# The second block of 256 rows of an attention output stage: the plain form replaced by seven products

## The chip, the cores and the metric

The kernel runs on one core of a Trainium2 chip. The metric is the device time of the program in microseconds (us); three runs of the kernel before gave 1825.37, 1825.43 and 1826.04 us, with a median of 1825.43 us. A profile is one more execution, recorded by the hardware. Its engines are PE (TensorE, matmuls), PEld (its weight loads), DVE (VectorE), ACT (ScalarE), POOL (GpSimd) and SP (SyncE, which here only issues DMAs). L1521 means line 1521 of the kernel file.

## The reference, cut to what matters

The computation is a gated sum of an attention block and a mixture of small experts over 2048 tokens of width 1024:

```
qkv = x @ wqkv                       # 32 heads of 32
p   = softmax(q k^T / sqrt(32));  o = p v
a   = o.reshape(2048, 1024) @ wo     # the output projection
b   = sum over heads of gelu(x . u[e]) * v[e]   # e: one expert per head, by arg max
out = g * a + (1 - g) * b            # g = sigmoid(x . gate_w), one number per token
```

What the change touches is only the last step: `out`, rows by rows, from the unnormalised attention result `o`, a reciprocal per head and token (which has the gate in it), the weight `wo`, and a small second term (`at` times `vhl`) that carries `b`.

## The kernel before, in words

All large matmuls are made exact enough by splitting each float32 operand into a rounded high part and a low remainder; a product is then three matmuls, high with high, high with low and low with high. ACT makes the high part (a copy with rounding, L95) and DVE subtracts it from the operand to get the low part (L96). This pair is the function `split`.

The output stage works on eight blocks of 256 rows (`W = 256`), n = 0 to 7. For a block, `load_o` brings the attention result in as the tile `OC[n]` (128 partitions by 8 slices `kc` by 256 rows, in the pool `vpool`, name `V`, two buffers), and `load_rb` the reciprocals as `RB[n]` (name `accd`, two buffers; for block 0 the tile `rb0`). DVE multiplies the two (`scale_o`, L1575, or `split_o`, L1590).

There are two forms of the product of a block with `wo`:

- The plain form, `wo_mm`: for each of the 8 slices `kc`, three operand pairs by two row halves by two column halves, 12 matmuls (L1521), so 96 for a block, and 8 more matmuls (`av_mm`, L1528) for the second term. Blocks 0 and 1 use it. Its operands are `OH[n]` and `OL[n]` (tiles `z` and `acc`) and `woh[kc]`, `wol[kc]`.
- The form by seven products (Strassen-Winograd), `unit(n)`, for blocks 2 to 7. The block is cut into A11, A12, A21, A22 and the weight into B11 to B22. Seven products of 12 matmuls (`ht.product`, L964) and the same 8 matmuls of the second term, 92 in all. The operands are A11, A12, A22 and the sums S1 to S4 of rows, each 128 by 512, each made by `ht.operand`: for S1 to S4 a DVE sum (L946), then ACT high (L95) and DVE low (L96). On the weight's side they are B11, B21, B22, which lie in `woh` and `wol`, and T1 to T4, high and low parts of 1 MiB each, which were computed earlier, stored in device memory (`TD`) and loaded by `load_t`. P1 to P7 use the pairs (A11,B11), (A12,B21), (S4,B22), (A22,T4), (S1,T1), (S2,T2), (S3,T3). The results are added by DVE (`tt`, L970) in `post` (four slots of 512 columns; `post` is the tile `rb0` again) and in `c1`, and stored.

`unit(n)` also prepares the operands of block n + 1 (`ahead`) while PE works on block n, and loads block n + 2. P1 of the next block is the first to need them. PSUM has eight banks, taken in turn.

The order is written out by hand: every engine runs its instructions in the order of the program text, and no scheduler moves them. SP issues all loads and stores of this stage in that order too, so a DMA that has to wait for a buffer or for data holds back every DMA behind it. For the last attention head the row sums go to device memory and come back as reciprocals: `load_r` (rr from smd), `norm_r` (a reciprocal, then a store rd from rr), and then `load_chunk(n, KC - 1, KC)` loads the last slice (kc = 7) of o and of the reciprocals for blocks 0 and 1. PE does the slices 0 to 6 of block 0 in the meantime.

`plain_out(n, pa)` empties the four banks of a plain block into the four slots of `post`, DVE and ACT in turn, and issues one store of 256 KB from each slot.

Of the kernel before, what the change touches and what calls it, by code (L numbers as in the profile page):

```python
# [10 lines left out]
F32R = mybir.dt.float32r  # L11
# [5 lines left out]
S = 2048  # L17
D = 1024
H = 32
KC = D // 128  # L20
HC = KC // 2
# [3 lines left out]
W = 256  # L25
# [6 lines left out]
def gated_mha_peer_kernel(ctx, tc, xT, wqkv, wv, wo, wq, k12, ug, v, out):  # L32
# [869 lines left out]
    zp = Pool("zp", side="right")  # L902
# [66 lines left out]
    def tt(out, a, b, op=OP.add):  # L969
        nc.vector.tensor_tensor(out=out, in0=a, in1=b, op=op)  # L970
# [279 lines left out]
    keep = Pool("keep")  # L1250
# [157 lines left out]
    def load_o(n, k0, k1, queue=nc.sync):  # L1408
        if k0 == 0:
            OC[n] = vpool.tile([128, KC, W], F32, name="V")  # L1410
        dma(OC[n][:, k0:k1, :], OD[n // 2, :, :, n % 2, k0:k1, :].rearrange("d j g s -> (d j) g s"), queue)

    def load_rb(n, k0, k1, queue=nc.sync):
        if k0 == 0:
            RB[n] = rb0 if n == 0 else wk.tile([128, KC, W], F32, name="accd")
        src = RD[:, n, k0:k1, :].rearrange("j g s -> j (g s)")[None]
        dma(RB[n][:, k0:k1, :].rearrange("p g s -> p (g s)"),
            src.to_broadcast([32, 4, (k1 - k0) * W]), queue)
# [83 lines left out]
    fin = Pool("fin")  # L1502
# [9 lines left out]
    def load_at(n):  # L1512
        AT[n] = fin.tile([128, W], F32R, name="at", bufs=3)
        dma(AT[n], ATD[:, n * W:(n + 1) * W])

    def wo_mm(pa, n, kcs, first, last):
        for kc in kcs:
            wh, wl = (W0[0][:, 0], W0[0][:, 1]) if n == kc == 0 else (woh[kc], wol[kc])
            for a, b, i in ((OH[n], wh, 0), (OH[n], wl, 1), (OL[n], wh, 2)):
                for tt, half in pa:  # L1520
                    nc.tensor.matmul(pa[tt, half], a[:, kc, tt * 128:(tt + 1) * 128],  # L1521
                                     b[:, half * 512:(half + 1) * 512],
                                     start=(first and kc == kcs[0] and i == 0),
                                     stop=(last and kc == kcs[-1] and i == 2))

    def av_mm(n, tt, half, ps, first=False, last=False):
        for i in range(2):
            nc.tensor.matmul(ps, AT[n][:, tt * 128:(tt + 1) * 128],  # L1528
                             vhl[:, i, half * 512:(half + 1) * 512],
                             start=(first and i == 0), stop=(last and i == 1))  # L1530
# [8 lines left out]
    def store(n, tt, half, r, c=slice(0, 512)):  # L1539
        dma(out[n * W + tt * 128:n * W + (tt + 1) * 128, half * 512 + c.start:half * 512 + c.stop],  # L1540
            r[:, c])
# [18 lines left out]
    def load_t(i, *parts):  # L1560

        ops = ht.b.setdefault(f"T{i + 1}", [None, None])
        for n, (part, src) in enumerate(zip(parts, TD[i])):
            if part is None:
                continue
            m = HC // len(part)
            for j, place in enumerate(part):
                dma(place, src[:, m * j:m * j + m, :].rearrange("p k m -> p (k m)"))
            ops[n] = [place[:, k * 512:(k + 1) * 512] for place in part for k in range(m)]

    def scale_o(n):

        for k in range(2):
            o = OC[n][:, k * HC:(k + 1) * HC]
            nc.vector.tensor_mul(o, o, RB[n][:, k * HC:(k + 1) * HC])  # L1575
        ht.rows(OC[n])
# [3 lines left out]
    def plain_out(n, pa):  # L1580
        for i, ((j, half), ps) in enumerate(pa.items()):
            if i % 2:
                nc.scalar.activation(post[:, i], ps, AF.Copy)
            else:
                nc.vector.tensor_copy(post[:, i], ps)
            store(n, j, half, post[:, i])

    def split_o(n, k0, k1):
        o = OC[n][:, k0:k1, :]
        nc.vector.tensor_mul(o, o, RB[n][:, k0:k1, :])  # L1590
        split(OH[n][:, k0:k1, :], OL[n][:, k0:k1, :], o)

    def banks4():
        return {(i, half): bank() for i in range(W // 128) for half in range(2)}
# [8 lines left out]
    for kc in range(1, KC - 1):  # L1603
        split_hi(kc + 1)
        if kc == 1:
            norm_sums(H - 1, sm, nc.scalar)
            load_r(G - 1)
            for n in range(2):
                load_at(n)
            load_o(1, 0, KC - 1)  # L1610
            pso.close()
        split_lo(kc)
        wo_mm(pa, 0, [kc], False, False)
        if kc == HC:
            norm_r(G - 1)
    for n in range(2):
        load_chunk(n, KC - 1, KC)
    load_rb(2, 0, KC)
    split_lo(KC - 1)
    split(woh[0], wol[0], raw_wo(0))  # L1620

    load_t(2, None, [fin.tile([128, S], F32R, name="t3l")])
    OH[1] = zp.tile([128, KC, W], F32R, name="z1")
    OL[1] = wk.tile([128, KC, W], F32R, name="acc")
    split_o(1, 0, HC)
    split_o(0, KC - 1, KC)
    load_o(2, 0, KC)
    load_t(0, *([keep.tile([128, S], F32R, name=f"wo_raw{j}")] for j in range(2)))  # L1630
    ps_odd = Pool("ps_odd", space=PSUM)
    for (i, half), ps in pa.items():
        av_mm(0, i, half, ps)
    wo_mm(pa, 0, [KC - 1], False, True)
    split_o(1, HC, KC)
    load_at(2)
    load_t(2, [zp.tile([128, S], F32R, name="z0")], None)
    load_t(1, *([keep.tile([128, S], F32R, name=f"wo_raw{2 + j}")] for j in range(2)))
    load_rb(3, 0, KC)
    load_o(3, 0, KC)  # L1640
    pa1 = banks4()
    wo_mm(pa1, 1, list(range(KC - 1)), True, False)
    for (i, half), ps in pa1.items():
        av_mm(1, i, half, ps)
    plain_out(0, pa)
    load_t(3, *([part[k][:, 512:] for k in range(HC)] for part in (woh, wol)))
    ht.places(wk.tile([128, S], F32R, name="acc"), "A11", "A12")
    ht.places(fin.tile([128, S], F32R, name="s31"), "S3", "S1")
    scale_o(2)
    for name in ("A11", "S3", "S1", "A12"):  # L1650
        ht.operand(name)
    wo_mm(pa1, 1, [KC - 1], False, True)
    ht.places(zp.tile([128, S], F32R, name="z1"), "S2")
    ht.places(wk.tile([128, S], F32R, name="acc"), "S4", "A22")
    load_at(3)
    ht.b.update({f"B{i + 1}{j + 1}": [[part[i * HC + k][:, j * 512:(j + 1) * 512] for k in range(HC)]
                                    for part in (woh, wol)] for i in range(2) for j in range(2)})

    def osb():
        return wk.tile([128, 512], F32, name="osb")  # L1660
# [1 line left out]
    def unit(n):  # L1662


        u2, u3, u5 = (post[:, i] for i in range(3))
        last = n == S // W - 1

        def ahead(*names):
            if last:
                return  # L1670
            for name in names:
                if name == "A11":
                    scale_o(n + 1)
                ht.operand(name)

        p1 = ht.product("P1")
        c1 = osb()
        nc.scalar.activation(c1, p1, AF.Copy)
        if n == 2:
            ht.operand("S2")  # L1680
            plain_out(1, pa1)
            for name in ("S4", "A22"):
                ht.operand(name)
        if n + 2 < S // W:
            load_chunk(n + 2, 0, KC)
            load_at(n + 2)
        ahead("A11")
        p7 = ht.product("P7")
        ahead("S3")
        p5 = ht.product("P5")  # L1690
        ahead("S1")
        p6 = ht.product("P6")
        tt(u2, c1, p6)
        tt(u3, u2, p7)
        tt(u2, u2, p5)
        tt(u5, u3, p5)
        ahead("S2")

        def c11():
            p2 = ht.product("P2", lambda ps: av_mm(n, 0, 0, ps, first=True))  # L1700
            pieces = 2 if last else 1
            for i in range(pieces):
                c = slice(i * 512 // pieces, (i + 1) * 512 // pieces)
                tt(c1[:, c], c1[:, c], p2[:, c])
                store(n, 0, 0, c1, c)

        def c12():
            p3 = ht.product("P3", lambda ps: av_mm(n, 0, 1, ps, first=True))
            tt(u2, u2, p3)
            store(n, 0, 1, u2)  # L1710

        def c22():
            ps = bank()
            av_mm(n, 1, 1, ps, True, True)
            tt(u5, u5, ps)
            store(n, 1, 1, u5)

        def c21():
            p4 = ht.product("P4", lambda ps: av_mm(n, 1, 0, ps, first=True))
            tt(u3, u3, p4)  # L1720
            store(n, 1, 0, u3)

        if not last:
            c11()
            ahead("A12")
        c12()
        ahead("S4")
        c22()
        c21()
        ahead("A22")  # L1730
        if last:
            c11()

    for n in range(2, S // W):
        unit(n)
    ps_odd.close()
    ps_even.close()
# [33 lines left out]
```

## Time and profile before

| what | value |
|---|---|
| median of the three runs | 1825.43 us |
| the profiled execution's own time | 1824.19 us |
| its span, first to last instruction | 1822.4 us |
| PE busy in the span | 1814.7 us (100%) |
| DVE, ACT busy | 1461.8 us (80%), 1312.8 us (72%) |
| granted TensorE clock | 1.00 |
| PE on the plain block 1 (104 matmuls) | about 23.6 us, ending at 1693.1 us |
| PE on one block by seven products (92 matmuls) | about 20.85 us |

Times inside the trace count from the span's start. A row of the timeline gives the start, the duration, the engine, the line, the operation, the tiles as out<-in, the count, and in brackets the idle time of the engine before it with what ended it. "SPq" rows are SP issuing a DMA: the time is that of the issue, not of the transfer. In a row of the windows view each engine has its busy time and count, then come the granted clock (PEclk), the mean busy share of the 16 DMA engines and what they moved in GB/s.

### The profile page before, as it was taken

To read this page: it belongs to the slowest core of one execution; us is meant where nothing else is said; L and a number is where in the kernel's file an instruction comes from. 1 tells how busy PE (TensorE), PEld (TensorE's weight loads), DVE (VectorE), ACT (ScalarE), POOL (GpSimd) and SP (SyncE) were. 2 spreads that over 40 slices of the span, in tenths; PEclk is the share of its full clock that TensorE was granted. 3 is DMA by queue.
4 is the path that set the end of the run, shared out by engine and by line. 5 is a ranking of instruction groups with operands and counts; after the bars stand their busy time and mean duration, and the time that the engine had idled before them with its cause. 6 is when DMAs were issued, how large, how long until landed. Compare 5 with 4: busy or idle time off the path is not lost.

```text
span 1822.4 us, 26410 instructions
## 1 busy us (share of the span) xinstructions
PE 1814.7 (100%) x10083; PEld 1099.5 (60%) x10083; DVE 1461.8 (80%) x1258; ACT 1312.8 (72%) x1716; POOL 227.5 (12%) x351
## 2 busy tenths in 40 slices
PE   9999999999999999999999999999999999999999
PEld 6777777788888644444444444444444444447887
DVE  7865876689967888888888888888888888897674
ACT  5544544532333699999999999999999999994221
POOL 1222222244101100000000000000000000000000
PEclk9999999999999999999999999999999999999999
DMA  7888689560267778777788878878787777866641
GB/s 268 277 280 277 215 291 292 191 224 13 81 231 239 232 161 183 157 168 167 166 173 174 181 163 178 171 171 185 165 182 168 163 167 179 185 149 243 252 156 58
DMA packets 117504, 345.23 MB, mean 189 GB/s; under 512 B 16160, under 2 KB 50112, under 8 KB 96448
## 3 DMA queue, kind: packets, MB, share of 16 engines
q1 hardware_dynamic: 87176, 195.37, 36.0%
q0 software_dynamic: 27888, 145.00, 34.4%
q10 hardware_dynamic: 2312, 3.15, 0.5%
q8 instruction: 80, 1.31, 0.3%
q14 instruction: 48, 0.39, 0.1%
HBM read 171.76 MB, written 72.36 MB: 134 GB/s over the span
## 4 chain that ended last, share of the span: by engine, by line
PE 94%; issue 2%; DVE 2%; DMA 1%; ACT 0%; POOL 0%; ACTq 0%; SPq 0%; DVEq 0%; POOLq 0%
PE ring L1318 29%; PE o L1339 26%; PE bk L303 15%; PE pa L964 6%; PE bk L725 5%; PE pa L1521 2%; PE bk L983 2%; PE bk L291 2%; PE bk L964 2%; PE bk L342 2%; PE ring L1352 1%; PE pa L1528 1%; DVE xh L970 1%; DMA t1l<-xl 0%; PE bk L191 0%
## 5 line engine op out<-in xcount | busy, mean ns | idle before, releaser
L1328 ACT ACTIVATE P<-ring 128x1024 f32<-128x1024 f32 (+2 forms) x1031 | 913.0, 984 | 13.3
L1368 DVE TENSOR_TENSOR acc<-acc,P 128x2048 f32<-128x2048 f32 x319 | 731.0, 2292 | 73.3 <-ACT P L1328 48.0
L1339 PE MATMUL o<-P,V 128*32 128x512 f32 x3840 | 464.8, 599 | 0.0
L1318 PE MATMUL ring<-Q,K 98*128 98x512 f32 x1024 | 271.7, 407 | 0.1
L1318 PE MATMUL ring<-z,z 98*128 98x512 f32 x1020 | 270.5, 407 | 0.6 <-ACT accd L1328 0.6
L1318 PEld LDWEIGHTS ring<-Q,K 98*128 98x128 f32 x1024 | 182.2, 188 | 143.6 <-ACT P L1328 73.5
L1318 PEld LDWEIGHTS ring<-z,z 98*128 98x128 f32 x1020 | 181.6, 188 | 142.3 <-ACT P L1328 72.3
L1339 PEld LDWEIGHTS o<-P,V 128*32 128x32 f32 x3840 | 99.0, 109 | 223.3 <-issue 214.4
L1361 POOL DMA_DIRECT2D accd<-P x95 | 81.5, 858 | 928.6 <-PE ring L1318 321.6
L1366 DVE TENSOR_TENSOR acc<-P,P 128x2048 f32<-128x2048 f32 x32 | 73.4, 2293 | 73.8 <-ACT P L1328 73.8
L303 PE MATMUL bk<-xh,A 128*128 128x512 f32 x336 | 82.8, 396 | 0.0
L303 PE MATMUL bk<-xh,S 128*128 128x512 f32 x336 | 81.3, 393 | 0.0
L303 PE MATMUL bk<-xl,S 128*128 128x512 f32 x336 | 80.1, 391 | 0.0
L136 ACT ACTIVATE hi<-u 128x512 fp32r<-128x512 f32 x42 | 26.6, 632 | 70.2 <-issue 39.7
L303 PEld LDWEIGHTS bk<-xh,A 128*128 128x128 f32 x336 | 62.1, 188 | 23.8 <-issue 5.9
L1371 DVE TENSOR_TENSOR acc<-acc,accd 128x2048 f32<-128x2048 f32 x32 | 73.1, 2285 | 0.0
L303 PEld LDWEIGHTS bk<-xl,S 128*128 128x128 f32 x336 | 62.8, 188 | 16.3 <-issue 2.5
L303 PEld LDWEIGHTS bk<-xh,S 128*128 128x128 f32 x336 | 62.4, 188 | 14.5 <-issue 1.7
L1328 ACT ACTIVATE accd<-ring 128x1024 f32<-128x1024 f32 (+2 forms) x64 | 62.3, 1034 | 2.3 <-PE ring L1318 2.2
L964 PE MATMUL pa<-woh,acc 128*128 128x512 f32 x192 | 62.2, 389 | 0.0
L512 DVE TENSOR_TENSOR u<-u,bk 128x512 f32<-128x512 f32 x70 | 46.7, 683 | 10.0 <-DMA wpd<-u 5.6
L729 ACT ACTIVATE xu<-bk 128x64 f32<-128x64 f32 x16 | 3.6, 222 | 61.1 <-PE bk L725 61.1
(301 smaller groups left out, 2209.3 us busy)
## 6 DMA issues: line engine op xcount, KB each, us to landing
accd<-P POOLq DMA_DIRECT2D x95, 1024.0 KB, 7.8
wqt<-in_wq SPq DMA_DIRECT2D x64, 512.0 KB
wraw<-in_wqkv SPq DMA_DIRECT2D x28, 512.0 KB
kdh<-hi POOLq DMA_DIRECT2D x32, 256.0 KB, 5.3
kdl<-lo POOLq DMA_DIRECT2D x32, 256.0 KB, 6.5
qdh<-hi POOLq DMA_DIRECT2D x32, 256.0 KB, 6.0
qdl<-lo POOLq DMA_DIRECT2D x32, 256.0 KB, 5.8
z<-kdh SPq DMA_DIRECT2D x32, 256.0 KB
```

The costliest lines, as they stand in the source:

```text
L291: nc.tensor.matmul(b0[w, n], AW[PLAIN[w, ki]][a][:, k, :], X[f"B{ki + 1}{n + 1}"][b][:, k, :], start=first, stop=last)
L303: nc.tensor.matmul(ps, a[i][:, k, :], b[j][:, k, :], start=(k == 0 and i == j == 0), stop=(k == HC - 1 and i == 1))
L512: nc.vector.tensor_tensor(out=out, in0=a, in1=b, op=OP.add)
L725: nc.tensor.matmul(ps, x_part(a, t // 4, kc)[:, tok], b, start=first, stop=last)
L964: nc.tensor.matmul(ps, self.a[a][i][:, k, :], self.b[b][j][k], start=(not first and k == 0 and i == j == 0), stop=(k == HC - 1 and i == 1))
L1318: on_ring(nc.tensor.matmul(ring[:, i, :], K[:98, kt * 128:(kt + 1) * 128], Q[:98, qc * 512:(qc + 1) * 512], start=True, stop=True), i)
L1328: on_ring(nc.scalar.activation(P[h, kt][:, q0 * 512:(q0 + m) * 512].rearrange("p (a m) -> p a m", a=m), ring[:, i:i + m, :], AF.Exp, scale ...
L1339: nc.tensor.matmul(O[h][32 * qc:32 * qc + 32, :], Vt[g][:, kt, 32 * j:32 * j + 32], p[:, qc * 512:(qc + 1) * 512], start=(kt == 0), stop=( ...
L1361: nc.gpsimd.dma_start(ACCD[h], P[h, kt], accum_op=OP.add)
L1366: nc.vector.tensor_add(ACC[h], P[h, 0], P[h, kt])
L1368: nc.vector.tensor_add(ACC[h], ACC[h], P[h, kt])
L1371: nc.vector.tensor_add(ACC[h], ACC[h], ACCD[h])
```

## The change

Block 1 is computed by `unit(1)` instead of the plain form. For that:

- The low part of T3 is loaded earlier, in the loop over the slices of block 0 at kc = 1, behind the load of block 1's slices 0 to 6. The high part of T3 goes to the buffer `z1`, and T1, T2 and this part of T3 are loaded before the reciprocals and the o of block 2. T4 is loaded right after those and `at` of block 2. All this is the order on SP's queue.
- Block 1's operands A11 and S3 are made before the last slice of block 0 is scaled and split, A12 and S1 after it. S2, S4 and A22 follow inside `unit(1)`, after its first product.
- `plain_out(0, pa)` comes after the loads of T4.
- The closing sum of the first quarter (`c11`, P2) comes right after P1 in `unit(1)`. Since `c1` is still needed there, its result goes to `post[:, 3]` for n = 1, and to `c1` as before for the others.

```diff
@@ in the loop over the slices of block 0, at kc == 1
             load_o(1, 0, KC - 1)
+            load_t(2, None, [fin.tile([128, S], F32R, name="t3l")])
             pso.close()
...
-    load_rb(2, 0, KC)
     split_lo(KC - 1)
     split(woh[0], wol[0], raw_wo(0))
-    load_t(2, None, [fin.tile([128, S], F32R, name="t3l")])
-    OH[1] = zp.tile([128, KC, W], F32R, name="z1")
-    OL[1] = wk.tile([128, KC, W], F32R, name="acc")
-    split_o(1, 0, HC)
+    load_t(2, [zp.tile([128, S], F32R, name="z1")], None)
+    load_t(0, *([keep.tile([128, S], F32R, name=f"wo_raw{j}")] for j in range(2)))
+    load_t(1, *([keep.tile([128, S], F32R, name=f"wo_raw{2 + j}")] for j in range(2)))
...
+    ht.places(wk.tile([128, S], F32R, name="acc"), "A11", "A12")
+    ht.places(fin.tile([128, S], F32R, name="s31"), "S3", "S1")
+    scale_o(1, 0)
+    for name in ("A11", "S3"):
+        ht.operand(name)
     split_o(0, KC - 1, KC)
+    load_rb(2, 0, KC)
     load_o(2, 0, KC)
-    load_t(0, *([keep.tile([128, S], F32R, name=f"wo_raw{j}")] for j in range(2)))
     ps_odd = Pool("ps_odd", space=PSUM)
     for (i, half), ps in pa.items():
         av_mm(0, i, half, ps)
     wo_mm(pa, 0, [KC - 1], False, True)
-    split_o(1, HC, KC)
+    scale_o(1, 1)
+    for name in ("A12", "S1"):
+        ht.operand(name)
     load_at(2)
-    load_t(2, [zp.tile([128, S], F32R, name="z0")], None)
-    load_t(1, *([keep.tile([128, S], F32R, name=f"wo_raw{2 + j}")] for j in range(2)))
-    load_rb(3, 0, KC)
-    load_o(3, 0, KC)
-    pa1 = banks4()
-    wo_mm(pa1, 1, list(range(KC - 1)), True, False)
-    for (i, half), ps in pa1.items():
-        av_mm(1, i, half, ps)
+    load_t(3, *([part[k][:, 512:] for k in range(HC)] for part in (woh, wol)))
     plain_out(0, pa)
-    load_t(3, *([part[k][:, 512:] for k in range(HC)] for part in (woh, wol)))
...
-    scale_o(2)
-    for name in ("A11", "S3", "S1", "A12"):
-        ht.operand(name)
-    wo_mm(pa1, 1, [KC - 1], False, True)
-    ht.places(zp.tile([128, S], F32R, name="z1"), "S2")
+    ht.places(zp.tile([128, S], F32R, name="z0"), "S2")
     ht.places(wk.tile([128, S], F32R, name="acc"), "S4", "A22")
-    load_at(3)
@@ in unit(n)
+        def c11():
+            p2 = ht.product("P2", lambda ps: av_mm(n, 0, 0, ps, first=True))
+            pieces = 2 if last else 1
+            r = post[:, 3] if n == 1 else c1
+            for i in range(pieces):
+                c = slice(i * 512 // pieces, (i + 1) * 512 // pieces)
+                tt(r[:, c], c1[:, c], p2[:, c])
+                store(n, 0, 0, r, c)
+
         p1 = ht.product("P1")
         c1 = osb()
         nc.scalar.activation(c1, p1, AF.Copy)
-        if n == 2:
-            ht.operand("S2")
-            plain_out(1, pa1)
-            for name in ("S4", "A22"):
+        if n == 1:
+            for name in ("S2", "S4", "A22"):
                 ht.operand(name)
         if n + 2 < S // W:
             load_chunk(n + 2, 0, KC)
             load_at(n + 2)
+        if n == 1:
+            c11()
         ahead("A11")
         p7 = ht.product("P7")
...
         if not last:
-            c11()
+            if n > 1:
+                c11()
             ahead("A12")
...
-    for n in range(2, S // W):
+    for n in range(1, S // W):
         unit(n)
```

More of the change, by code (lines that the diff above doesn't have):

```diff
@@ L1569, in load_t, with scale_o @@
             ops[n] = [place[:, k * 512:(k + 1) * 512] for place in part for k in range(m)]
-    def scale_o(n):
-        for k in range(2):
+    def scale_o(n, *ks):
+        for k in ks or range(2):
             o = OC[n][:, k * HC:(k + 1) * HC]
@@ L1617, in gated_mha_peer_kernel @@
         load_chunk(n, KC - 1, KC)
-    load_rb(2, 0, KC)
     split_lo(KC - 1)
     split(woh[0], wol[0], raw_wo(0))
-    load_t(2, None, [fin.tile([128, S], F32R, name="t3l")])
-    OH[1] = zp.tile([128, KC, W], F32R, name="z1")
-    OL[1] = wk.tile([128, KC, W], F32R, name="acc")
-    split_o(1, 0, HC)
+    load_t(2, [zp.tile([128, S], F32R, name="z1")], None)
+    load_t(0, *([keep.tile([128, S], F32R, name=f"wo_raw{j}")] for j in range(2)))
+    load_t(1, *([keep.tile([128, S], F32R, name=f"wo_raw{2 + j}")] for j in range(2)))
+    ht.b.update({f"B{i + 1}{j + 1}": [[part[i * HC + k][:, j * 512:(j + 1) * 512] for k in range(HC)]
+                                    for part in (woh, wol)] for i in range(2) for j in range(2)})
+    ht.places(wk.tile([128, S], F32R, name="acc"), "A11", "A12")
[3 more added lines that the diff above has]
+        ht.operand(name)
     split_o(0, KC - 1, KC)
+    load_rb(2, 0, KC)
     load_o(2, 0, KC)
-    load_t(0, *([keep.tile([128, S], F32R, name=f"wo_raw{j}")] for j in range(2)))
     ps_odd = Pool("ps_odd", space=PSUM)
@@ L1634, in gated_mha_peer_kernel @@
     wo_mm(pa, 0, [KC - 1], False, True)
-    split_o(1, HC, KC)
+    scale_o(1, 1)
+    for name in ("A12", "S1"):
+        ht.operand(name)
     load_at(2)
-    load_t(2, [zp.tile([128, S], F32R, name="z0")], None)
-    load_t(1, *([keep.tile([128, S], F32R, name=f"wo_raw{2 + j}")] for j in range(2)))
-    load_rb(3, 0, KC)
-    load_o(3, 0, KC)
-    pa1 = banks4()
-    wo_mm(pa1, 1, list(range(KC - 1)), True, False)
-    for (i, half), ps in pa1.items():
-        av_mm(1, i, half, ps)
-    plain_out(0, pa)
-    load_t(3, *([part[k][:, 512:] for k in range(HC)] for part in (woh, wol)))
-    ht.places(wk.tile([128, S], F32R, name="acc"), "A11", "A12")
-    ht.places(fin.tile([128, S], F32R, name="s31"), "S3", "S1")
-    scale_o(2)
-    for name in ("A11", "S3", "S1", "A12"):
-        ht.operand(name)
-    wo_mm(pa1, 1, [KC - 1], False, True)
-    ht.places(zp.tile([128, S], F32R, name="z1"), "S2")
+    load_t(3, *([part[k][:, 512:] for k in range(HC)] for part in (woh, wol)))
+    plain_out(0, pa)
+    ht.places(zp.tile([128, S], F32R, name="z0"), "S2")
     ht.places(wk.tile([128, S], F32R, name="acc"), "S4", "A22")
-    load_at(3)
-    ht.b.update({f"B{i + 1}{j + 1}": [[part[i * HC + k][:, j * 512:(j + 1) * 512] for k in range(HC)]
-                                    for part in (woh, wol)] for i in range(2) for j in range(2)})
     def osb():
@@ L1697, in unit @@
         ahead("S2")
[L1699 to L1705, printed above, removed]
         def c12():
```

## The prediction

> **What bounds the kernel now.** I read the page first, then the chain of waits over the last 220 us.
>
> ```profile
> span 1822.4 us, 26410 instructions
> PE 1814.7 (100%) x10083; PEld 1099.5 (60%) x10083; DVE 1461.8 (80%) x1258; ACT 1312.8 (72%) x1716; POOL 227.5 (12%) x351
> ```
>
> ```profile
> 1667.00 21.76 PE pa L1521 x96
> 1688.76 1.81 PE pa L1528 x8
> 1690.57 2.72 PE pa L1521 x12
> 1693.29 6.80 PE pa L964 x30
> ```
>
> PE is the chain, without a hole. The row of 96 matmuls holds block 0's last slice (12) and 84 of block 1; with 8 and 12 more, block 1 costs 104. Twelve take 2.72 us, 0.227 us each. A stage of which PE is never idle gets shorter by the matmuls taken out, as long as everything else stays in time. So the question is what else becomes late, and for that the order on the DMA queue and on DVE matters. The timeline of SP (first fence) and of DVE and ACT (second), then the windows view:
>
> ```profile
> 1652.47 0.38 SPq L77 DMA_DIRECT2D V<-od  x1
> 1655.72 0.59 SPq L77 DMA_DIRECT2D rd<-rr  x1
> 1659.07 0.54 SPq L77 DMA_DIRECT2D rb<-rd  x1
> ...
> 1661.62 0.54 SPq L77 DMA_DIRECT2D t3l<-t2l  x1
> 1666.00 0.33 SPq L77 DMA_DIRECT2D V<-od  x1
> 1666.38 0.43 SPq L77 DMA_DIRECT2D wo_raw<-t0h  x1
> ...
> 1675.56 0.34 SPq L77 DMA_DIRECT2D out<-rb  x1
> ```
>
> ```profile
> 1661.15 1.22 DVE L1590 TENSOR_TENSOR V<-V,accd 128x1024 f32<-128x1024 f32 x1
> ...
> 1664.65 0.42 DVE L1590 TENSOR_TENSOR V<-V,rb 128x256 f32<-128x256 f32 x1
> 1665.10 0.42 ACT L95 ACTIVATE z<-V 128x256 fp32r<-128x256 f32 x1 [1.63 <-DVE V L1590]
> ...
> 1666.61 0.87 PEld L1521 LDWEIGHTS pa<-woh,z 128*128 128x128 f32 x4
> 1666.84 1.07 PE L1521 MATMUL pa<-woh,z 128*128 128x512 f32 x4
> ...
> 1669.38 1.28 DVE L1585 COPY rb<-pa 128x512 f32<-128x512 f32 x2
> ...
> 1673.15 2.36 DVE L1575 TENSOR_TENSOR V<-V,accd 128x1024 f32<-128x1024 f32 x2 [2.49 <-DMA V<-od]
> ```
>
> ```profile
> 1657.00:1660.00 3.00, 3.00 (x15) 2.49 (x14) 3.00 (x5) 1.38 (x2) 0.00 (x0) 1.00 0.23 63
> ...
> 1672.50:1680.00 7.50, 7.50 (x35) 6.21 (x34) 5.45 (x7) 2.42 (x4) 0.00 (x0) 1.00 1.02 427
> 1680.00:1688.00 8.00, 8.00 (x37) 6.64 (x36) 1.30 (x3) 0.00 (x0) 0.00 (x0) 1.00 1.01 424
> 1688.00:1696.00 8.00, 8.00 (x37) 6.64 (x36) 0.00 (x0) 0.00 (x0) 0.00 (x0) 1.00 1.01 395
> ```
>
> The reader should see three things. The DMA engines are full (share 1.0, 395 to 427 GB/s) from 1672.5 to 1696 us. What is issued waits its turn: block 2's o, issued at 1666.00 behind t3l among others, lets DVE start only at 1673.15. And these late transfers cost nothing today, because 23.6 us of plain matmuls, whose operands are in place, run over them. The change takes away this cover.
>
> **Term 1, matmuls.** Block 1 goes from 104 to 92: minus 12 x 0.227 = **-2.72 us**. PE would start block 1 at 1669.56 (1666.84 + 2.72) and, unhindered, block 2 at 1690.4 in place of 1693.13.
>
> **Term 2, operands moved ahead of block 0's last slice.** On DVE, A11 and S3 of block 1 now come between the multiply at 1661.15 and the one at 1664.65. These rows price an operand of 512 columns (sum, high, low):
>
> ```profile
> 1699.01 0.68 DVE L946 TENSOR_TENSOR V<-V 128x512 f32<-128x512 f32 x1
> 1699.72 1.16 ACT L95 ACTIVATE acc<-V 128x512 fp32r<-128x512 f32 x2 [1.58 <-DVE V L946]
> 1700.39 1.30 DVE L96 TENSOR_TENSOR acc<-V,acc 128x512 fp32r<-128x512 f32 x2 [0.70 <-ACT acc L95]
> 1701.60 2.36 DVE L1575 TENSOR_TENSOR V<-V,accd 128x1024 f32<-128x1024 f32 x2
> 1702.90 0.64 ACT L95 ACTIVATE acc<-V 128x512 fp32r<-128x512 f32 x1 [2.02 <-issue]
> 1703.87 0.69 DVE L96 TENSOR_TENSOR acc<-V,acc 128x512 fp32r<-128x512 f32 x1
> ```
>
> Multiply to 1662.4; A11 high on ACT to 1663.0, low on DVE to 1663.75; sum S3 to 1664.4, high to 1665.0, low to 1665.75. Then the small multiply (0.42) and ACT (0.42) end at 1666.55, and PE's weight load at 1666.61 just finds it. Cost 0; 0 to 0.5 us if it slips, and a slip here is absorbed by the idle time of term 4. A12 and S1 follow (1.22, then some 0.8 and 2.0 us) and are there by 1672.5; PE wants A12 at 1672.7 and S1 at 1678. S2, S4 and A22 take about 5 us more of DVE and end near 1678.5, before PE asks for them (1681 and later). Cost 0, covered by P1, P2, P7 and P5.
>
> **Term 3, transfers.** T3's low part now sits on the queue at about 1652.9, ahead of the small store rd<-rr (1655.72), whose landing releases rb<-rd (1659.07) and all behind it. The store waits for 1 MiB: at 425 GB/s 2.47 us, at the least nothing (the window 1657 to 1660 is nearly empty, 63 GB/s). I take **2.0 us**, near the upper end, because the store lands behind everything issued earlier. The last slice of block 0 still comes in time: DVE reaches it about 1 us later than before, its reciprocals come 2 us later, and before they were issued 5.6 us ahead of their use.
>
> Behind these small loads the new order is T3 high, T1 (2), T2 (2), reciprocals and o of block 2, `at`, T4 (2), then the four stores of `plain_out(0)`: 10.125 MiB. Before, the third MiB of that stream (reciprocals, T3 low, o) was usable at 1673.15. From the third to the end are 4.125 MiB in long rows at 425 GB/s (10.2 us) and 3 MiB of T4 and stores at 395 GB/s (8.0 us). So T1 is there near 1675 (wanted 1678), T2 near 1680 (wanted 1681), T4's eight pieces from 1686 to 1691 (its first low piece near 1688.5, wanted near 1688): little or no room, up to 1 us of waiting in P4, which term 4 absorbs. The last store has let go of its slot at 1673.15 + 18.2 + 2.0 = **1693.3**.
>
> **Term 4, the wait that is added.** `c11` of block 1 writes `post[:, 3]`, which the last of these stores still reads. DVE comes to it at 1678.5 and stands until 1693.3. No PE work of block 1 waits for that, but behind `c11` on DVE stand block 2's multiplies and operands. From 1693.3: the sum 0.61 (back to back, 1.30 - 0.69 above), multiplies from 1693.9, A11 high on ACT at +1.30 for 0.64, then 0.05 and the 0.23 from weight load to matmul: PE starts block 2 at **1696.1**. A11 low begins at multiply + 2.27 and takes 0.69, so the third matmul runs at 1697.1 and P1 ends its 12 at 1699.4. Before: 1693.13 + 2.72 = 1695.85. That is +3.55. P5 needs a bank that DVE frees by block 1's second closing sum, which comes after S3, S1 and one other sum, 8.8 us behind `c11`: 1702.1 plus the weight load, against 1699.4 + 2.72: +0.2. **Sum +3.75 us**, which holds the -2.72 already: about 6.5 us of new waits. Later blocks run at PE's pace again: DVE is busy some 15 of 21 us a block.
>
> ```profile
> 1734.80:1755.60 20.80, 20.80 (x93) 17.22 (x92) 14.99 (x22) 4.80 (x8) 0.00 (x0) 1.00 0.42 159
> ```
>
> The profiled execution took 1824.19 us with a span of 1822.4; the median of the runs is 1.24 us above. The difference is put on the median: 1825.43 + 3.75 = **1829.2 us** (+0.21%).
>
> **The clock as a cost of the hole.** In term 4 PE is idle from about 1691 to 1696, and before it never was. The only row with an idle PE is the end of the program:
>
> ```profile
> 1818.40:1821.00 2.60, 0.01 (x1) 0.00 (x0) 0.75 (x2) 0.00 (x0) 0.00 (x0) 1.00 0.29 101
> 1821.00:1822.40 1.40, 0.00 (x0) 0.00 (x0) 0.00 (x0) 0.00 (x0) 0.00 (x0) 0.52 0.00 0
> ```
>
> After 2.6 us of idleness the granted clock falls to half. So it may fall in this hole too. The cost is 0 if it is back at the first matmul, and 2.72 less the 0.8 of waits inside P1 and before P5, so 1.9, if P1 runs wholly at half. I count 0 in the sum, because which it is depends on a phase that no row shows. [...]
>
> **The rivals.**
> (A) The stores don't hold DVE, being done before it matters. `c11` by 1687.6 (1690.4 less the 2.8 to a ready A11) keeps all of the gain: 1825.43 - 2.72 = 1822.7. Break-even is `c11` at 1689.5. For it: the stores are 1 MiB in all, ready at 1674. Against it: before, the first of them was issued only at 1675.56, 6 us after its data was copied (1669.38), with less ahead of it. Chance 0.15.
> (B) T3's early load holds nothing up, since it fills the empty window: `c11` at 1691.3, 2.0 less: 1827.2. Chance 0.13.
> (C) The clock falls and stays down into P1: 1829.2 + 1.2 = 1830.4, between its ends. Chance 0.22.
> (D) The stream is slower than the rows, 395 GB/s all the way and the full 2.47 us: +0.8 and +0.5, and the late T4 or the small loads cost another 0.5 to 1: about 1831.3. Chance 0.10.
>
> **How the numbers follow.** The forecast itself, 1829.2, has 0.40; its own range is 1827.2 (the lower end of term 3) to 1831.9 (0.8 of a slower stream and 1.9 of the clock). The range for 8 in 10 must reach down to (A), so 1822.5, and up into (D), 1831.9. A change of 0.2% (3.65 us) is about what a measurement of this kernel can tell from none: below 1821.8 is faster, above 1829.1 slower. The forecast lies just past that bound, so I give 0.23 of its 0.40 to slower and 0.17 to the same; (A) and (B) are the same, with 0.02 taken for faster; (C) and (D) are slower, with 0.01 given back. Faster 0.02, same 0.44, slower 0.54.
>
> **What would show it.** Right: DVE idle for some 15 us from about 1678, ended by a store of `out` from rb; PE's first matmul of block 2 near 1696, its wait ended by ACT's high part of A11; P1 to P4 of block 1 unbroken from 1669.6 but for a microsecond near T4; rb<-rd issued near 1661; a clock below 1.00 around 1696 for (C). Wrong: DVE closing c11 by 1688, or PE waiting inside block 1 for longer than it waits after it.

## The result, and the profile after

| | median (us) | lowest to highest | runs |
|---|---|---|---|
| before | 1825.48 | 1825.23 to 1827.08 | 7 |
| after | 1832.43 | 1830.04 to 1833.15 | 7 |

The ratio is 1.0034, with a 95% interval of 1.0025 to 1.0043: the change makes the kernel slower, by 6.95 us between the medians. The profiled execution took 1832.55 us, with a span of 1830.8 us, 8.4 us more than the one of before. The next figures show that not all of that is the change's. The chain of waits of both kernels has the first twelve matmuls of the output stage and the last twelve of the kernel. Before:

```profile
1642.96 2.95 PE pa L1521 x12
...
1815.69 2.73 PE pa L964 x12
```

After, with what lies between (start, duration, what):

```profile
1645.30 2.94 PE pa L1521 x12
...
1669.33 2.72 PE pa L1521 x12
...
1675.22 4.97 PE pa L964 x22
1680.20 11.44 DMA woh<-t3h
...
1691.70 5.18 DMA out<-rb
...
1697.59 1.95 DVE V L1575 x2
...
1700.60 11.93 PE pa L964 x46
...
1824.05 2.73 PE pa L964 x12
```

From the first of these rows to the last the stage took 172.73 us before and 178.75 us after: **6.02 us more**. The other 2.34 us already stood when the stage began, in work that the change does not touch. In the thirteen profiles of this study the stage began anywhere from 1642.9 to 1645.7. I call "stage" the time between these two rows from here on; it is free of that scatter.

The chain no longer runs through PE alone. It goes back from block 2's first product to DVE, from there to a store of `out` from rb, and from there along SP's queue to a piece of T4. The rows of the timeline behind it, first the release of block 0's last reciprocals on SP, then PE, DVE and ACT:

```profile
1663.62 0.54 SPq L77 DMA_DIRECT2D rb<-rd  x1
...
1690.03 0.40 PE L964 MATMUL pa<-woh,acc 128*128 128x512 f32 x1
1692.31 0.50 PE L964 MATMUL pa<-wol,acc 128*128 128x512 f32 x1 [1.89 <-DMA wol<-t3l]
...
1696.98 0.69 DVE L970 TENSOR_TENSOR rb<-osb,pa 128x512 f32<-128x512 f32 x1 [16.11 <-DMA out<-rb]
1697.59 2.35 DVE L1575 TENSOR_TENSOR V<-V,accd 128x1024 f32<-128x1024 f32 x2
...
1698.84 0.63 ACT L95 ACTIVATE acc<-V 128x512 fp32r<-128x512 f32 x1 [18.77 <-DVE V L1575]
1699.52 0.59 PE L964 MATMUL pa<-woh,acc 128*128 128x512 f32 x1 [2.84 <-ACT acc L95]
...
1704.20 0.40 PE L964 MATMUL pa<-z,s 128*128 128x512 f32 x1
```

DVE stands 16.11 us in `c11` for the store. PE, which had no hole before, waits 1.89 us inside P4 for T4 and 2.84 us before block 2. Block 1 started at 1671.89; its 92 matmuls of 0.2267 us would have ended at 1692.75, and block 2 starts at 1699.52: 6.77 us of holes and slow matmuls. P1 of block 2 then takes 4.68 us until P7 at 1704.20, where twelve matmuls need 2.72: another 1.96. Together 8.73, less the 2.72 of the twelve matmuls saved, is the 6.01 that the stage shows. The windows view gives the clock, in stretches cut where it changes:

```profile
1689.55:1692.96 3.41, 1.52 (x7) 0.86 (x5) 0.00 (x0) 0.00 (x0) 0.00 (x0) 1.00 1.05 405
1692.96:1696.38 3.42, 3.42 (x10) 2.54 (x8) 0.00 (x0) 0.00 (x0) 0.00 (x0) 0.50 1.07 396
1696.38:1699.79 3.41, 0.57 (x3) 0.27 (x2) 2.81 (x3) 0.63 (x1) 0.00 (x0) 1.00 1.01 386
1699.79:1703.20 3.41, 3.35 (x8) 2.15 (x8) 2.65 (x5) 0.63 (x1) 0.00 (x0) 0.50 0.47 184
```

The granted clock was halved twice, once after each hole.

### The profile page after: what moved, and what is told of

It is laid out like the page before. It is cut to its first block, busy times and chain, and to the rows that moved or that the text cites. A ratio compares the mean times of both kernels' runs of the same rounds, so it can differ in the third digit from the quotient of the medians.

```text
span 1830.8 us, 26413 instructions
## 1 busy us (share of the span) xinstructions
PE 1817.5 (99%) x10071; PEld 1098.4 (60%) x10071; DVE 1470.0 (80%) x1273; ACT 1314.1 (72%) x1720; POOL 227.6 (12%) x351
## 4 chain that ended last, share of the span: by engine, by line
PE 92%; DMA 3%; DVE 2%; issue 2%; POOL 0%; ACT 0%; SPq 0%; DVEq 0%; POOLq 0%; ACTq 0%
PE ring L1318 28%; PE o L1339 26%; PE bk L303 15%; PE pa L964 7%; PE bk L725 5%; PE bk L983 2%; PE bk L291 2%; PE bk L342 2%; PE ring L1352 1%; PE pa L1521 1%; PE bk L964 1%; PE pa L1528 1%; DMA xl<-in_wo 1%; DMA woh<-t3h 1%; DVE xh L970 1%
## 5 line engine op out<-in xcount | busy, mean ns | idle before, releaser
L964 PE MATMUL pa<-woh,acc 128*128 128x512 f32 x224 | 75.1, 400 | 2.9 <-ACT acc L95 2.8
L303 PEld LDWEIGHTS bk<-xl,S 128*128 128x128 f32 x336 | 62.8, 188 | 16.3 <-issue 2.5
L95 ACT ACTIVATE acc<-V 128x512 fp32r<-128x512 f32 x28 | 17.1, 626 | 54.9 <-DVE V L1575 25.9
```

The lines of the kernel that those rows point to most:

```text
L303: nc.tensor.matmul(ps, a[i][:, k, :], b[j][:, k, :], start=(k == 0 and i == j == 0), stop=(k == HC - 1 and i == 1))
L964: nc.tensor.matmul(ps, self.a[a][i][:, k, :], self.b[b][j][k], start=(not first and k == 0 and i == j == 0), stop=(k == HC - 1 and i == 1))
```

## The experiments

My theory after the result: DVE's wait for the slot of `post` is the main cost (W), with the late T4 and the halved clock behind it. The main rival: the DMA stream as a whole is late, so that taking away one wait uncovers the next (D). All runs, with the stage read from each profile in the way shown above (one profile a run), and each median beside that of the kernel before on the same chip:

| run | stage, us against before's 172.73 | median (us) | before beside it | ratio, 95% interval |
|---|---|---|---|---|
| after_again | +5.88 | 1831.79 | 1825.72 | 1.0040, 1.0026 to 1.0054 |
| e1_own_slot | +1.05 | 1826.66 | 1825.72 | 1.0004, 0.9995 to 1.0013 |
| e2_stores_pool | +3.60 | 1828.60 | 1825.72 | 1.0019, 1.0010 to 1.0028 |
| e3_fill | +5.72 | 1831.54 | 1825.72 | 1.0034, 1.0021 to 1.0048 |
| f1_early_slot | +3.21 | 1827.03 | 1825.25 | 1.0009, 1.0000 to 1.0019 |
| f2_early | +1.74 | 1826.48 | 1825.25 | 1.0006, 0.9997 to 1.0015 |
| g1_slot_fill | -0.48 | 1825.12 | 1825.25 | 1.0000, 0.9991 to 1.0009 |
| h1_first_slot | -1.14 | 1824.57 | 1825.65 | 0.9995, 0.9986 to 1.0004 |
| h2_first | +0.68 | 1826.55 | 1825.65 | 1.0005, 0.9996 to 1.0014 |
| h3_o_t3l_first | -2.72 | 1822.77 | 1825.74 | 0.9984, 0.9975 to 0.9993 |
| h4_t3l_first | -2.61 | 1823.25 | 1825.74 | 0.9987, 0.9978 to 0.9996 |

### after_again: the changed kernel once more

> The changed kernel once more, as the base for the three others on the same chip. Its first profile ran 8.4 us longer than the one before, of which 2.3 us already stood when the output stage began (PE's first matmul of it at 1645.30 against 1642.96), in work that the change does not touch. Theory 1 (those 2.3 us are the execution's own, and differ from run to run): this profile begins the output stage at another time, and the time is 6 to 7 us over the kernel before. Theory 2 (the change moves something early): the output stage again begins near 1645.3.

The stage began at 1644.01 in this profile, and took 178.61 us, within 0.14 of the first. So theory 1 holds: the start is the execution's own, the stage is the change's. The median is 6.07 us over that of the kernel before, close to the 5.88 of the stage.

### e1_own_slot: c11 without the slot

```diff
-            r = post[:, 3] if n == 1 else c1
+            r = osb() if n == 1 else c1
```

> c11 of block 1 gets a tile of its own in place of the fourth slot of post; nothing else changes. Theory W (DVE's wait for the last store of block 0 is what costs): DVE does c11 about 3 us after block 1's P2, its next wait is the load of block 2's o, A11 of block 2 is ready before PE has ended block 1, and what is left is PE's wait in P4 for T4 with the halved clock after it: 4 to 5.5 us faster than the changed kernel, so 1 to 2.5 us over the kernel before. Rival D (the DMA stream as a whole is late, and the wait for the store only sits in front of waits just as long, for block 2's o and its other stores): at most 2 us faster than the changed kernel.

Measured: 5.1 us faster than the changed kernel in the median, 4.83 in the stage. W, not D. The timeline of DVE in this run:

```profile
1679.94 0.68 DVE L970 TENSOR_TENSOR osb<-osb,pa 128x512 f32<-128x512 f32 x1
1688.16 2.36 DVE L1575 TENSOR_TENSOR V<-V,accd 128x1024 f32<-128x1024 f32 x2 [7.55 <-DMA V<-od]
```

`c11` runs as soon as A22 is made. DVE then waits 7.55 us for block 2's o, but that wait ends early enough. What is left of the loss is PE in P4, in its timeline and windows:

```profile
1691.39 0.50 PE L964 MATMUL pa<-wol,acc 128*128 128x512 f32 x1 [1.81 <-DMA wol<-t3l]
```

```profile
1692.50:1696.00 3.50, 3.50 (x10) 2.75 (x9) 2.69 (x5) 0.63 (x1) 0.00 (x0) 0.51 1.07 378
```

1.81 us of waiting and then 3.4 us at half clock (1.7 us lost) are 3.5; less the 2.72 saved, 0.8 against the measured 1.05.

### e2_stores_pool: block 0's four stores from another engine

```diff
-            store(n, j, half, post[:, i])
+            store(n, j, half, post[:, i], queue=nc.gpsimd)
```

> The four stores of block 0 are issued by POOL in place of SP; c11 keeps its slot in post. Theory W: these stores no longer stand behind T4, DVE's wait for them ends within 3 us after A22 of block 1 is made, and its cost goes. T4 and block 2's o come up to 2.5 us later, since the 1 MiB of stores now goes ahead of them, so PE's wait in P4 grows from 1.9 us to 2 to 4.4 us. In all 1.5 to 4 us faster than the changed kernel. Rival D: as much is lost in P4 as is gained, within 1 us of the changed kernel.

Measured: 3.2 us faster than the changed kernel, so W again; where the stores stand in the queue matters. But one number missed: the wait for the store did not end within 3 us, it fell from 16.1 only to 7.3. The DMA engines were full all the while (398 to 425 GB/s from 1676 to 1692 us), and other transfers were late. The timeline shows PE waiting for T2 (`wo_raw<-t1l`), DVE for the store and for block 2's o, and PE for both parts of T4:

```profile
1681.80 2.79 PE L964 MATMUL pa<-wo_raw,z 128*128 128x512 f32 x11 [0.63 <-DMA wo_raw<-t1l]
1685.90 0.69 DVE L970 TENSOR_TENSOR rb<-osb,pa 128x512 f32<-128x512 f32 x1 [7.30 <-DMA out<-rb]
1689.05 2.36 DVE L1575 TENSOR_TENSOR V<-V,accd 128x1024 f32<-128x1024 f32 x2 [2.46 <-DMA V<-od]
1690.04 0.47 PE L964 MATMUL pa<-woh,acc 128*128 128x512 f32 x1 [1.37 <-DMA woh<-t3h]
1692.39 0.50 PE L964 MATMUL pa<-wol,acc 128*128 128x512 f32 x1 [1.89 <-DMA wol<-t3l]
```

So D holds in part: in this run the new order changed which transfer was late.

### e3_fill: the clock in P1 of block 2

```diff
+        if n == 2:
+            ps = bank()
+            bank_no[0] -= 1
+            for _ in range(12):
+                nc.tensor.matmul(ps, AT[1][:, :128], vhl[:, 0, :512], start=True, stop=True)
         p1 = ht.product("P1")
```

> Twelve extra matmuls stand between block 1 and block 2 on PE, into the bank that P1 of block 2 then overwrites (their result is not used); they take 2.7 us and fit into PE's wait for A11. Theory C (the halved clock in P1 of block 2 costs 2 us of its own): the clock stays at 1.00 after the wait and the time falls by 1.5 to 2.2 us against the changed kernel. Rival (P1 is paced by the low part of A11 and by the banks anyway, so the clock costs nothing): no change, or up to 1 us slower because the extra matmuls reach past the wait.

Theory C does not hold. The windows view shows that the clock stayed at 1.00 after the wait, and the timeline that P1 now waits for other things:

```profile
1698.70:1702.00 3.30, 2.72 (x11) 1.91 (x11) 2.54 (x4) 0.90 (x2) 0.00 (x0) 1.00 0.63 252
```

```profile
1699.02 0.50 PE L964 MATMUL pa<-woh,acc 128*128 128x512 f32 x1 [0.24 <-ACT acc L95]
...
1700.09 0.73 PE L964 MATMUL pa<-woh,acc 128*128 128x512 f32 x2 [0.34 <-DVE acc L96]
...
1705.62 3.00 PE L964 MATMUL pa<-wo_raw,s 128*128 128x512 f32 x12 [0.25 <-DVE rb L970]
```

The stage fell by only 0.16 us against after_again, the median by 0.25. P1 took 3.47 us, where it took 4.43 in after_again, so 0.96 less. But from P7 to the end of P6 PE took 8.87 us, where it took 8.17: P5 now waited for a bank that DVE's sums free, and 0.70 us of the gain went again. Behind the hole PE follows DVE, and a slow P1 loses little that PE would not have waited anyway.

### g1_slot_fill: the clock in P4 of block 1

To e1_own_slot:

```diff
+            if n == 1:
+                ps = bank()
+                bank_no[0] -= 1
+                for _ in range(8):
+                    nc.tensor.matmul(ps, AT[1][:, :128], vhl[:, 0, :512], start=True, stop=True)
             p4 = ht.product("P4", lambda ps: av_mm(n, 1, 0, ps, first=True))
```

> As e1_own_slot, with eight extra matmuls (1.8 us) ahead of P4 of block 1, into the bank that P4 then overwrites; they stand where PE would wait for T4 (1.81 us in e1). Theory C2 (there the fall of the clock to half is a cost of its own, because P4 and then P1 follow without a break): the clock stays at 1.00 through P4 and P1, and the time falls by 1.2 to 1.8 us against e1_own_slot. Rival: the clock makes no difference, or the extra matmuls cost what they save: within 0.6 us of e1_own_slot.

The stage is 1.53 us shorter than that of e1, as C2 has it; against their own runs of before the medians differ by 1.07 us, a little less than C2 said and more than the rival allows. C2 holds. The chain of waits has no DMA in it any more, only eight extra matmuls (L1715) in the place of the hole. The 60 matmuls behind them take 13.69 us; in the kernel before, with the clock at 1.00, 60 such matmuls took 13.60:

```profile
1689.41 1.83 PE pa L1715 x8
...
1692.02 13.69 PE pa L964 x60
```

T4 is no earlier than in e1: the first matmul with its low part starts 47.1 us after the stage's first matmul, in e1 46.9. So the fall of the clock cost 0.2 us in one place and 1.5 in the other. In these two runs it cost where PE was the bound right after the hole.

### f1_early_slot and f2_early: T3 and T1 earlier, from another engine

f1 to e1_own_slot, f2 to the changed kernel (`load_t` has got a queue as an argument):

```diff
@@ at kc == 1
-            load_t(2, None, [fin.tile([128, S], F32R, name="t3l")])
+            load_t(2, [zp.tile([128, S], F32R, name="z1")], [fin.tile([128, S], F32R, name="t3l")],
+                   queue=nc.gpsimd)
@@ in the loop over kc
+        if kc == 2:
+            load_t(0, [keep.tile([128, S], F32R, name="wo_raw0")], None, queue=nc.gpsimd)
+        if kc == HC:
+            load_t(0, None, [keep.tile([128, S], F32R, name="wo_raw1")], queue=nc.gpsimd)
@@ after the loop
-    load_t(2, [zp.tile([128, S], F32R, name="z1")], None)
-    load_t(0, *([keep.tile([128, S], F32R, name=f"wo_raw{j}")] for j in range(2)))
```

> As e1_own_slot, and T3 (both parts) and T1 are loaded by POOL, T3 at slice 1, T1 at slices 2 and 4, as soon as their buffers are free. Theory L (e1 still loses its gain because 3 MiB of T3 and T1 stand on SP's queue ahead of block 2's o and of T4): the DMA engines take these 4 MiB in the half-empty stretch before, T4 and block 2's o come 5 to 7 us earlier, PE has no wait left in P4, and the whole gain of 12 matmuls shows: 1 to 3.2 us faster than the kernel before, 2 to 4 us faster than e1_own_slot. Rival Q (the early 4 MiB push the small store and loads of the last head back, whichever queue they are issued from): block 0's last slice waits for them, and the time is that of the kernel before or worse.

> As f1_early_slot, but c11 keeps its slot in post, as in the changed kernel. Theory L: block 0's four stores now have 3 MiB less in front of them and land 6 to 8 us earlier, DVE's wait for the last of them ends some 8 us after A22 instead of 16, A11 of block 2 is just in time, and the time is within 1 us of f1_early_slot. Rival: the wait for the slot stays a cost of its own, 2 us or more over f1_early_slot.

Rival Q holds for f1. Its chain of waits, PE's timeline, and the clock:

```profile
1650.46 4.90 DMA smd<-ssb
1655.37 3.82 DMA rr<-smd
...
1670.93 5.49 PE pa L1521 x12
```

```profile
1670.93 2.08 PE L1521 MATMUL pa<-woh,z 128*128 128x512 f32 x4 [2.73 <-ACT z L95]
```

```profile
1670.20:1677.00 6.80, 6.07 (x14) 4.84 (x15) 4.41 (x8) 2.71 (x5) 0.00 (x0) 0.50 0.97 395
```

The last head's row sums go out at 1650.46 and come back as a load that SP can only issue 4.90 us later; before, these two issues were 1.76 us apart (1649.32 on ACT, 1651.08 on SP). PE waits 2.73 us in block 0's last slice, and the clock is halved for 6.8 us. What stands behind that is as theory L had it: no wait in block 1, and none at the start of block 2. In f2 the hole is as long (2.74 us), but the clock was low for 3.4 us only. That is why f2's stage is shorter than f1's though it keeps the slot. f1's profile is also the slowest of its eleven runs (1828.54 us against a median of 1827.03). In f2's trace the slot cost nothing: DVE's wait for the store is 7.48 us, close to the 8 expected, and ends 6.0 us before PE is through with block 1; PE does not wait behind it. The medians, f2 0.55 us below f1, are within the 1 us that theory L gave.

### h1 to h4: early loads in the right place

The DMA engines are nearly idle at the start of the output stage, before the row sums are stored. In the kernel before they moved 3 GB/s there:

```profile
1646.00:1649.00 3.00, 3.00 (x26) 0.93 (x19) 3.00 (x5) 1.93 (x4) 0.00 (x0) 1.00 0.01 3
```

h1 (to e1_own_slot) and h2 (to the changed kernel) issue block 1's o and T3 there:

```diff
@@ behind finish(H - 1), ahead of the loop
+    load_o(1, 0, KC - 1)
+    load_t(2, [zp.tile([128, S], F32R, name="z1")], [fin.tile([128, S], F32R, name="t3l")])
@@ at kc == 1
-            load_o(1, 0, KC - 1)
-            load_t(2, None, [fin.tile([128, S], F32R, name="t3l")])
@@ after the loop
-    load_t(2, [zp.tile([128, S], F32R, name="z1")], None)
```

> As e1_own_slot (c11 with a tile of its own), and the loads of block 1's o (slices 0 to 6) and of both parts of T3 are issued by SP at the start of the output stage, ahead of its wait for the last head's row sums, while the DMA engines are nearly idle. Theory L2 (the transfers are late only because they stand in the same stretch as the small loads of the last slice; f1 failed because its 4 MiB stood across them): the small store and loads go as in the kernel before, the stream behind them starts 2 us earlier and has 1 MiB less in it, PE has no wait in block 1 and none before block 2, the clock stays at 1.00, and the time is 2.2 to 3.2 us under the kernel before. Rival Q2 (the 3 MiB still reach into the small store, or wait for their buffers and hold SP): PE waits in block 0's last slice, 0 to 4 us over the kernel before.

> As h1_first_slot, but c11 keeps its slot in post. Theory W with L2: block 0's stores land some 4.5 us earlier than in the changed kernel, near the point (2.8 us ahead of PE's end of block 1) from which the wait for the slot costs; so 0 to 2.5 us over h1_first_slot, and at least 3 us faster than the changed kernel. Rival (the slot costs nothing once the stream is early): within 0.5 us of h1_first_slot.

h1 lies between its theory and its rival: block 1 and block 2 run without a hole, but the 3 MiB still reach into the small transfers (5.11 us from the store of the row sums to the next issue), and PE waits 1.29 us in block 0's last slice:

```profile
1670.99 1.20 PE L1521 MATMUL pa<-woh,z 128*128 128x512 f32 x4 [1.29 <-ACT z L95]
```

The clock did not fall there in this profile: it was 1.00 from 1665 to 1675 us. In this run's own time the DMA engines moved 399 GB/s from 1653.5 to 1656.5 us and 69 GB/s behind that; the next small load was issued at 1657.15. (The text on h3 below says that the 3 MiB ended near 1653.5; in this trace it is 1656.5.) h2 is 2.0 us over h1 by the median, and 1.8 in the stage. Its DVE is released only 2.1 us before PE is through with block 1, and PE then waits for DVE and ACT in P1 and P5 of block 2:

```profile
1690.68 0.69 DVE L970 TENSOR_TENSOR rb<-osb,pa 128x512 f32<-128x512 f32 x1 [10.87 <-DMA out<-rb]
1693.22 0.50 PE L964 MATMUL pa<-woh,acc 128*128 128x512 f32 x1 [0.26 <-ACT acc L95]
```

So the slot costs something even with an earlier stream, as W had it.

h3 and h4 (both to e1_own_slot) take less ahead: h3 block 1's o and the low part of T3, h4 that part alone.

```diff
@@ behind finish(H - 1)
+    load_o(1, 0, KC - 1)              # h3 only
+    load_t(2, None, [fin.tile([128, S], F32R, name="t3l")])
@@ at kc == 1
-            load_o(1, 0, KC - 1)      # h3 only
-            load_t(2, None, [fin.tile([128, S], F32R, name="t3l")])
```

> As h1_first_slot, but of T3 only the low part goes ahead, behind block 1's o; the high part stands again behind the loads of the last slice. In h1 the 3 MiB ended only near 1653.5 us and held up the store of the last head's row sums, so PE waited 1.29 us in block 0's last slice. Theory L3 (it is the third MiB that reaches into that store): 2 MiB are through before the store is issued, PE has no wait there or one below 0.5 us, T4 is still in time, and the time is 1.7 to 2.8 us under the kernel before. Rival (any large load at the start holds that store up, or T4 is late again): PE waits 1 us or more in one of the two places, 1 us or less under the kernel before.

> As e1_own_slot, and T3's low part alone is issued at the start of the output stage; block 1's o stays where it was. Against e1_own_slot this takes just 1 MiB out of the way of the small store of the reciprocals. Theory S (this is the 2.2 us by which the release of rb<-rd came later than in the kernel before): rb<-rd is issued 16 to 17 us after the start of the output stage, as in the kernel before and not 18.4, T4 comes 2 us earlier, PE's wait in P4 falls from 1.81 us to below 0.5, and the time is 1.7 to 2.8 us under the kernel before. Rival (the release is late for another reason): as e1_own_slot.

Both theories hold. h3 is faster than the kernel before, 0.9984 (0.9975 to 0.9993), by 2.97 us in the medians, a little more than the 2.8 expected at most. From the stage's first matmul to the kernel's last its chain of waits is PE alone, and its stage is shorter by 2.72 us, the twelve matmuls to the hundredth:

```profile
1644.10 2.95 PE pa L1521 x12
...
1668.14 2.72 PE pa L1521 x12
1670.86 2.72 PE pa L964 x12
...
1688.99 13.60 PE pa L964 x60
...
1814.11 2.73 PE pa L964 x12
```

h4 is faster than the kernel before as well, 0.9987 (0.9978 to 0.9996), by 2.49 us in the medians and 2.61 in the stage, and its PE does not wait in P4. So moving the one MiB of T3's low part is enough. One row tells why, the release of the last slice's loads on SP:

```profile
1660.93 0.54 SPq L77 DMA_DIRECT2D rb<-rd  x1
```

That is 16.3 us after the stage's first matmul (1644.63), as before (1659.07 - 1642.96 = 16.1); in the changed kernel it was 18.3 (1663.62 - 1645.30).

## Why the prediction was right or wrong

The direction and the mechanism were right, the size too small: +3.75 us was forecast, +6.02 is what the stage shows, and 6.95 what the medians show. The median of 1832.43 lies 0.5 us above the range; that of the repeat, 1831.79, lies just inside it.

**Term 1** was right to the hundredth; h3 shows its 2.72 us with nothing else in the way.

**Term 2** cost nothing, as forecast: block 0's last slice runs unbroken from 1669.33.

**Term 3** was right in its first half. The release of rb<-rd came 2.2 us later, where I took 2.0, and h4 shows that the early load of T3 was the cause. Its second half was mis-sized. I had the last store let go of its slot at 1693.3, 50.3 us after the stage's first matmul; DVE was released at 1696.98, which is 51.7. 0.2 of these 1.3 us is the release of rb<-rd. A slower stream is not the reason: at its end it ran at 386 to 405 GB/s, where I had taken 395. The last of the stores, issued at 1691.70, landed 5.18 us later. Before it landed SP issued behind it block 3's o, its reciprocals and `at`, 2.2 MB, which my 10.125 MiB left out. From 1696.9 to 1709 the DMA engines moved only 1.72 MB in all, c11's store among it, so by an estimate some 0.8 MB of these loads, about 1.9 us at 400 GB/s, went before the store had landed. That this is the missing 1.1 us no run tests. T4 was late by 1.89 us, where I had said up to 1.

**Term 4** was the main step, and it was right in kind: 16.11 us of waiting in `c11` against 15 forecast, ended by the store, with PE's first matmul of block 2 waiting for ACT's high part of A11. e1 shows that this wait was worth 4.8 us. Its end was mis-sized: P1 of block 2 took 4.68 us until P7 could start, and I had 3.3. The later start (1.1) and the longer P1 (1.4), less 0.2 for the bank, which no longer held P5 up, make the missing 2.3 us. The later start is term 3's late release of DVE (1.3), less 0.3 because PE started 2.54 us behind that release and not 2.8.

**The clock.** I counted 0 in the sum and gave rival (C) 1.2. The fall happened, twice, and the longer P1 is its work. But e3 shows that the clock by itself is worth little there: with the clock kept at 1.00 P1 takes 3.47 us, near my 3.3, but PE then waits for the banks that DVE frees. That cost 0.70 us from P7 to the end of P6, where I had 0.2, and the stage falls by 0.16 us alone. What paces PE behind the hole is DVE, which has all operands of block 2 still to make. That the price depends on a phase was my guess, which no run tests. In the trace of the changed kernel the clock changed in steps of 3.41 us, at 1692.96, 1696.38, 1699.79 and 1703.20. The first fall came at the end of a stretch in which PE was busy for 1.52 of its 3.41 us, after a hole of 1.89; the second came after one of 2.84. At the end of the kernel before, in the row that I quoted, it fell 2.6 us after the last matmul.

**Rival (A)**, that the stores don't hold DVE, is excluded by the wait of 16.11 us and by e1. **(B)**, that T3's early load holds nothing up, is excluded by h4. **(D)** named one thing that did happen beside the forecast, a late T4; its slower stream did not show. In the changed kernel the late T4 was hidden behind the longer wait of DVE; once that was gone, in e1, it cost 3.5 us with the clock that fell behind it.

What stays open is where the missing 1.1 us of the store's landing arose. The 0.9 us by which the first medians differ more than the stage did not come again: in after_again the medians differ by 6.07 us and the stage by 5.88. So I put it down to the scatter of the stage's beginning, which is larger.

## What to carry to other kernels

When a stage that is bound by PE is shortened, look at what its length covered. Here 23.6 us of plain matmuls hid a DMA stream of nearly 10 MB; the form with fewer matmuls was worth its 2.72 us only after one result got a tile of its own and one MiB of loads (h4), or nearly two (h3), went to where the DMA engines were idle. Before a result is put into a slot that "is free by then", follow the last reader of that slot; if it is a store, count what is queued around it, not only its own 256 KB: here DVE stood 16.11 us for it. And look for large loads that stand across a chain of small dependent transfers: here they made PE wait 1.3 to 2.7 us, whether SP or POOL issued them.

## What the runs showed of the hardware that was not expected

- The halved clock did not cost the same in two places. The fall cost 0.2 us where PE was following another engine (e3) and 1.5 us where PE was the bound behind the hole (g1 against e1).
- In the profiles a hole of 1.8 to 1.9 us was followed by a fall of the clock (after, e1), one of 1.29 us (h1) was not; two holes of 2.7 us were followed by 6.8 us at half clock in one profile (f1) and 3.4 us in the other (f2). The same hole does not seem to have the same price in every run. f1's four runs with a mean clock of 1.000 took 1824.98 to 1826.28 us, its seven with 0.999 or 0.998 took 1826.92 to 1828.54; in e1 five of eleven list 1.000. This is a hint and no proof, for 3.4 us at half clock lower the mean by only 0.001, and 5 of 90 runs of the kernel before, which has no such hole, list 0.999 too.
- Issuing the large loads from another engine did not let the small transfers past: with them in flight, from the store of 8 KB to the issue of the load that depends on it were 4.90 us (f1, loads from POOL) and 5.11 us (h1, loads from SP), and 1.76 us without.
